# A fused attention and PReLU kernel under a new written order: 1,116 steps, their PSUM banks and the filler matmuls at other places

## The chip, the cores and the metric

The kernel runs on one core of a Trainium2 chip. The core has five engines that work side by side, each through its own instructions in program order: TensorE (PE in the profile, with its weight loads listed apart as PEld), VectorE (DVE), ScalarE (ACT), GpSimd (POOL) and SyncE (SP, which only issues transfers here). They wait for each other through semaphores. Matrix products land in PSUM, a small memory of eight banks; from there DVE or ACT moves them on. The metric is the device time of one execution in microseconds, and lower is better.

## The reference

For each of 8 batches and 8 heads, 512 tokens of width 64 attend to 32 states of the same width, and the states attend to the tokens. Both reads go through one PReLU layer pair of width 2048.

```python
def _attn_ref(x, state):            # x (8,8,512,64), state (8,8,32,64)
    scores = scale * x @ state.T;   a = softmax(scores);   xread = a @ state
    scores2 = scale * state @ x.T;  a2 = softmax(scores2); sread = a2 @ x
    return concatenate([xread, sread], axis=2)
...
    x = attn_out.transpose(0, 2, 1, 3).reshape(B * S, H * D)   # (4352, 512)
    h = x @ w_in                                               # (4352, 2048)
    g = maximum(h, 0) + alpha * minimum(h, 0)
    return g @ w_out                                           # (4352, 512)
```

## The kernel before

The work is cut into nine parts: batches 0 to 7 of 512 tokens each, and part 8, the 256 rows that the states have read. Inputs are turned to f16 on the way in; sums are f32 in PSUM.

**Attention of a batch b.** GpSimd loads x (`lx`, L163). SyncE transposes it by DMA (`xd`, L318); batches 0 and 1 are instead transposed on PE (`xt`) and copied out of PSUM (`xo`, L331). PE forms the scores of all heads (`sc`, L341). From that one PSUM tile DVE takes a block transpose (`sb`, L373) and a row maximum (`tm`, L456), and ACT two exponentials (`te`, L473). The first path is the tokens' softmax: maximum (`smax`), shift (`ssh`, on POOL), exponential (`sexp`), sum (`ssum`), scaling (`snorm`, L440), transpose back (`wb`, L443). The second is the states' softmax: scaling of the exponentials (`tn`, L489 on ACT or L491 on POOL), a DMA transpose by SyncE (`tt`, L495), the product with x on PE (`rd`, L510) and a copy into the rows of part 8 (`rdo`, L521). Batch 0 makes its token softmax from products with paired states instead (`tsc`, L380), in two halves, and transposes it on PE (`at`, L392; copied by `ao`, L395).

**First layer.** The states are multiplied by w_in first (`m`, L537, eight matmuls; copied out by `mo`, L561 or L563). A step `F.b.jc.k` (L590) multiplies that by the softmax weights: two matmuls 512 wide that give 128 of the 2048 hidden columns for all tokens of batch b, in PSUM bank k. ACT takes the negative part (`N`, L643), DVE combines it with the bank into g (`G`, L646), and only then is the bank free again. For part 8, `F` is four matmuls 256 wide (L599). The first two column blocks of batch 0 are done in halves (`f`, L612, `n`, `g`).

**Second layer.** Batch 0 is done plainly (`S`, L660, two matmuls 512 wide; `O` writes out). Parts 1 to 8 use seven products in place of eight for a two-by-two block product: sums of weight quarters (`W`, POOL, L704), sums of halves of g (`U`, POOL, L728, 2.1 us each), products (`P`, L749, four matmuls 256 wide) into three banks per part, partial results kept on the way (`K`, L765) and four quarters sent out (`Q`, L780 and L782, then two transfers by SyncE).

**Start.** DVE writes a pattern (`io`), and PE multiplies it by itself in filler steps (`Z`, L262; the last number counts units of 128 columns) while the first inputs arrive. The states of batch 0 come by `dst`, are turned to f16 by `stc`, transposed on PE into one PSUM tile (`stt`, L275), and that tile is read three times: `sto` (L289, the states as PE will use them) and `sbd.0`, `sbd.1` (L293, the paired states). Weights come in four chunks each (`wi`, `wo`, one transfer a chunk, issued by POOL).

**What sets the order.** Everything follows one text: `ORDER` lists all steps, and a loop at the end of the function calls them one after the other. Each engine runs its instructions in the order in which the list names them, and each queue of transfers likewise. A token gives the step, its batch and indices, then its PSUM banks (0 to 5; scores and some `m` use a further pair) or its engine (`a` ACT, `v` DVE, `p` POOL, `s` SP). So `F.6.2.0` is the first layer of batch 6, column block 2, in bank 0, and `Q.4.0.1.a` a quarter of batch 4 copied by ACT. The list comes from a planner, a program with assumed costs and due times; semaphore waits between the steps are set when the kernel is built, from what each step reads and writes.

Of the kernel before, what the change touches and what calls it, by code (L numbers as in the profile page):

```python
# [34 lines left out]
F.1.4.3 S.0.3.6 mo.1.2.a m.2.2.0.1 sc.2 G.1.6 S.0.3.4 sb.2 tt.0 N.1.4 F.1.8.4 mo.2.2.a.0 S.0.3.7 O.0.0.a mo.2.2.a.1
F.1.0.2 F.1.1.0 S.0.2.1.1 S.0.2.5 S.0.2.3 tm.2 smax.2 N.1.8 N.1.0 O.0.3.a G.1.8 S.0.2.4 nb.2.a S.0.2.6 F.1.13.5 G.1.4
G.1.0 te.2.0 W.3.1.p F.1.9.4 te.2.1 rd.0.3 N.1.1 W.4.0.p N.1.13 N.1.9 rd.1.2 m.3.2 W.4.1.p tsum.2 ssh.p.2 G.1.1
S.0.2.2 sexp.2 G.1.13 rdo.1.a S.0.2.7 S.0.2.0 rdo.0.v ssum.2.5 mo.3.2.a G.1.9 F.1.10.0 P.1.1.1.0.3 O.0.2.a tn.2.1.a
P.1.1.1.1 tn.2.0.a m.2.1 N.1.10 m.2.3.2.4 str.1.1 P.1.1.0.0 snorm.v.2 mo.2.3.a.1 F.1.11.5 lx.3 G.1.10 U.1.3.0.p
mo.2.3.a.0 U.1.1.1.p P.1.1.0.1 P.1.2.1.1.4 N.1.11 wb.2 mo.2.1.a G.1.11 tt.2 F.2.15.2 N.2.15 P.1.2.0.1 F.2.1.0 F.2.14.5  # L40
K.1.1.a sro.1.v P.1.2.1.0 m.3.1 G.2.15 U.1.2.1.p xd.3 N.2.1 m.3.0.1.2 G.2.1 N.2.14 mo.3.1.a P.1.2.0.0 U.1.1.0.p
mo.3.0.a.0 P.1.6.0.1 G.2.14 lx.4 F.2.0.0 N.2.0 U.1.2.0.p F.2.11.5 N.2.11 Q.1.0.0 F.2.2.4 mo.3.0.v.1 U.1.3.1.p
P.1.6.1.1 G.2.0 m.5.0.1.2 rd.2.0 sc.3 G.2.11 N.2.2 mo.5.0.a.0 mo.5.0.a.1 W.3.0.p m.4.0.5.1 G.2.2 P.1.6.0.0 P.1.6.1.0
rdo.2.v sb.3 mo.4.0.a.0 mo.4.0.a.1 K.1.2.a F.2.7.5 N.2.7 U.1.4.0.p tm.3 m.3.3.2.4 F.2.13.0 G.2.7 smax.3 mo.3.3.a.1
# [795 lines left out]
```

## Time and profile before

| | us |
|---|---|
| Median of 3 runs | 211.87 |
| Lowest and highest of them | 210.81, 213.03 |
| The profiled execution | 211.0 |
| Its span, from the first to the last instruction | 209.2 |
| Busy in the span: PE | 201.1 (96%) |
| DVE | 173.1 (83%) |
| POOL | 178.7 (85%) |
| ACT | 150.9 (72%) |
| Fillers on PE, busy | 10.5 |

The profile shows one execution. Rows of its timeline give start, length, engine, line, operation, tiles, shape and a count of instructions taken together; a bracket at the end gives the idle time before the row and who ended it. Matmuls overlap, and the end of each is modelled, so the time that a matmul costs PE is read from start to start of rows that follow each other, not from the lengths. The chain of waits is followed back from the last instruction. A wait is put down to the last semaphore that came, which need not be the whole cause.

### The profile page before, as it was taken

How to read it: one execution, taken by the hardware profiler on the slowest of the kernel's cores; microseconds unless marked ns; L12 is line 12 of the kernel's file. 1: busy time of each engine (PE TensorE's matmuls, PEld its weight loads, DVE VectorE, ACT ScalarE, POOL GpSimd, SP SyncE). 2: the span in 40 equal slices, each digit the busy share in tenths (PEclk: the TensorE clock that was granted, in tenths of full speed). 3: DMA queues.
4: the chain of work that ended last, by engine and by line, in shares of the span. 5: the costliest groups of instructions: out<-in, count | busy, mean ns of one | idle time of the engine just before them, and what ended most of it. 6: DMA issues, size and time to landing. Idle time of an engine off the chain costs nothing.

```text
span 209.2 us, 5084 instructions
## 1 busy us (share of the span) xinstructions
PE 201.1 (96%) x2009; PEld 134.5 (64%) x2009; DVE 173.1 (83%) x263; ACT 150.9 (72%) x295; POOL 178.7 (85%) x112
## 2 busy tenths in 40 slices
...
GB/s 142 190 171 165 205 200 147 211 143 75 218 110 155 48 127 213 22 11 238 199 112 140 113 126 26 3 77 119 109 2 3 125 25 3 50 50 53 115 114 124
DMA packets 44455, 23.43 MB, mean 112 GB/s; under 512 B 23696, under 2 KB 43920, under 8 KB 44432
## 3 DMA queue, kind: packets, MB, share of 16 engines
...
q8 instruction: 15, 0.25, 0.5%
...
## 4 chain that ended last, share of the span: by engine, by line
PE 73%; DVE 9%; DMA 8%; POOL 3%; issue 3%; ACT 2%; SPq 0%; DVEq 0%; POOLq 0%
PE px L749 21%; PE h L590 18%; PE pv L749 10%; PE o L660 6%; PE py L749 6%; DVE g L646 5%; DMA w_out_sb<-in_moe_w_out_dram 4%; PE m_ps L537 4%; PE h L599 3%; PE sr_ps L510 2%; DMA st<-in_state_dram 2%; DMA e2T<-e 2%; POOL gsum L728 2%; DVE nb L456 1%; POOL an L440 1%
## 5 line engine op out<-in xcount | busy, mean ns | idle before, releaser
L646 DVE SCALAR_TENSOR_TENSOR g<-neg,oma_sb,h 128x512 f16<-128x512 f32 (+1 forms) x142 | 94.9, 710 | 13.1 <-ACT neg L643 12.2
L643 ACT ACTIVATE neg<-h 128x512 f32<-128x512 f32 (+1 forms) x142 | 75.9, 583 | 23.8 <-PE h L590 13.3
L590 PE MATMUL h<-aT,m 128*128 128x512 f16 x252 | 66.8, 379 | 1.1 <-ACT oq L780 1.0
L749 PEld LDWEIGHTS <-gsum 128*128 128x128 f16 x480 | 46.5, 98 | 14.4 <-issue 1.5
L749 PEld LDWEIGHTS <-g 128*128 128x128 f16 x360 | 34.7, 98 | 10.5 <-issue 1.7
L728 POOL TENSOR_TENSOR gsum<-g,g 128x1024 f16<-128x1024 f16 (+1 forms) x16 | 32.1, 2009 | 7.1 <-DVE g L646 5.2
L590 PEld LDWEIGHTS <-m 128*128 128x128 f16 x252 | 24.2, 98 | 18.5 <-issue 2.6
L728 POOL TENSOR_TENSOR gsum<-g,gsum 128x1024 f16<-128x1024 f16 (+1 forms) x16 | 31.9, 2006 | 1.4 <-PE px L749 1.2
L728 POOL TENSOR_TENSOR gsum<-gsum,g 128x1024 f16<-128x1024 f16 (+1 forms) x16 | 32.1, 2008 | 1.0
L749 PE MATMUL px<-ws,gsum 128*128 128x256 f16 x240 | 32.1, 273 | 0.0
L728 POOL TENSOR_TENSOR gsum<-g 128x1024 f16<-128x1024 f16 (+1 forms) x16 | 32.1, 2013 | 0.0
L563 ACT CAST m<-m_ps 128x512 f16<-128x512 f32 x36 | 19.7, 596 | 2.7 <-PE m_ps L537 2.5
L765 ACT COPY kept<-px 128x512 f32<-128x512 f32 (+1 forms) x21 | 12.0, 570 | 13.0 <-PE px L749 12.9
L749 PE MATMUL px<-w_out_sb,g 128*128 128x256 f16 x120 | 17.4, 273 | 0.0
L749 PE MATMUL py<-w_out_sb,g 128*128 128x256 f16 x120 | 17.2, 273 | 0.0
L660 PE MATMUL o<-w_out_sb,g 128*128 128x512 f16 x64 | 16.5, 380 | 0.3 <-DMA w_out_sb<-in_moe_w_out_dram 0.3
L749 PE MATMUL px<-w_out_sb,gsum 128*128 128x256 f16 x120 | 16.7, 273 | 0.0
L749 PE MATMUL pv<-ws,gsum 128*128 128x256 f16 x120 | 16.5, 273 | 0.0
L749 PE MATMUL pv<-ws,g 128*128 128x256 f16 x120 | 15.9, 273 | 0.0
L411 POOL TENSOR_TENSOR ts<-ts,mx 128x1024 f32<-128x1024 f32 x7 | 13.4, 1913 | 2.5 <-DVE mx L406 2.5
L782 DVE TENSOR_TENSOR oq<-pv,kept 128x512 f32<-128x512 f32 (+1 forms) x16 | 10.4, 648 | 5.4 <-ACT kept L765 2.8
L561 ACT CAST m<-m_ps 128x1024 f16<-128x1024 f32 x12 | 12.5, 1045 | 0.0
...
## 6 DMA issues: line engine op xcount, KB each, us to landing
...
xg<-in_x_dram POOLq DMA_DIRECT2D x7, 512.0 KB, 6.3
w_in_sb<-in_moe_w_in_dram POOLq DMA_DIRECT2D x4, 512.0 KB, 9.4
w_out_sb<-in_moe_w_out_dram POOLq DMA_DIRECT2D x4, 512.0 KB, 8.4
...
```

Source lines behind the costliest of these rows:

```text
L411: engine(e).tensor_tensor(blocks(cols(live["ts", b], j, S)), blocks(scored(b, j)), over_blocks(cols(live["mx", b], j, S // N)), ALU.subtract,)
L537: nc.tensor.matmul(t[N * k : N * (k + 1), :], st_head(b, h)[64 * r : 64 * r + 64, :], w_in_sb[64 * r : 64 * r + 64, c, 512 * f : 512 * (f ...
L561: copier(e)(m_tile(b, f), t)
L563: copier(e)(m_tile(b, f)[:, g, :], t[g])
L590: nc.tensor.matmul(h_g, ms[b, f][:, g, 128 * j : 128 * (j + 1)], weights(b, g), start=(g == 0), stop=(g == 1),)
L643: nc.scalar.activation(neg, h, RELU, bias=0.0, scale=-1.0)
L646: nc.vector.scalar_tensor_tensor(g_tile(b, jc), negs.pop((b, jc)), oma_sb[:, jc : jc + 1], hs.pop((b, jc)), ALU.mult, ALU.add,)
L660: nc.tensor.matmul(outs[b, q], g_tile(b, jc)[:, 128 * q : 128 * (q + 1)], w_out_sb[:, jc, :], start=not begun and jc == 2 * jc2, stop=left ...
L728: engine(e).tensor_tensor(t, x(), y(), op)
L749: nc.tensor.matmul(pbanks[b, name][:, i, :], of(b, c)[:, j, 128 * i : 128 * (i + 1)], moving[:, 4 * c + j, :], start=not begun and j == 0, ...
L765: copier(e)(t, pbanks[b, "x"])
L782: nc.vector.tensor_tensor(osb, pbanks[b, name], kept[b, add], ALU.add)
```

## The change

Only the text `ORDER` changes; no function does. The planner wrote a new list. Its rules differ in two points: reads of one PSUM bank by different engines are taken to follow each other in program order, and the transfers that GpSimd and SyncE issue are taken to be served as one line. Nearly every step has another place, many another bank. Thirty steps change their engine: 14 go from DVE to ACT, 10 from ACT to DVE, four from ACT to POOL (`cx.0.1`, `tn.2.0`, `tn.2.1`, `tn.4.1`), one from POOL to ACT (`tn.3.0`) and one from POOL to DVE (`snorm.0.0`). The steps themselves are the same set, but for the fillers: eight with 138 units in all become nine with 162. Shown are the stretches that the text below speaks of.

```diff
--- before.py
+++ after.py
 ORDER = """
-dxp.1 io dx.0.0.4.s dx.0.4.8.a id lx.1 mz Z.4.38 dst.s stc.v cx.0.0.v stt.1 cx.0.1.a xt.0.0.1.3 sbd.0.v xt.0.0.0.0
-sbd.1.a xo.0.0.1.a Z.4.9 la sto.v tsc.0.1.5 xo.0.0.0.v tsc.0.0 xt.0.1.1.2 xt.0.1.0.0 smax.0.0 Z.4.15 xo.0.1.0.v
-xo.0.1.1.a tsc.1.1.3 ssh.v.0.0 tsc.1.0 Z.4.16 xt.1.1.1.5 sexp.0.0 smax.0.1 ssh.v.0.1 xt.1.0.0.2 ssum.0.0 xt.1.0.1.1
-lst.0 xt.1.1.0.0 xo.1.0.0.a wi.0 wi.1 sexp.0.1 xo.1.1.1.a xo.1.0.1.v snorm.p.0.0 str.0.3 Z.4.28 xo.1.1.0.v at.0.2
-ssum.0.1 sro.0.a sc.1 m.0.0.5.1 wi.2 snorm.p.0.1 oma.a ao.0.v sb.1 mo.0.0.a.1 m.1.0.0.3 wo.0 tm.1 mo.1.0.a.1
-mo.0.0.a.0 Z.4.21 at.1.1 m.2.0.3.2 mo.1.0.a.0 f.0.0.0.5 ao.1.v mo.2.0.a.0 Z.4.3 mo.2.0.v.1 nb.1.a wo.1 m.0.1.1.3
-n.0.0.0 mo.0.1.a.1 mo.0.1.v.0 f.0.0.1.0 g.0.0.0.1 F.0.3.2 n.0.0.1 g.0.0.0.0 F.0.5.3 F.0.7.1 N.0.3 g.0.0.1.0 wi.3 N.0.5
-g.0.0.1.1 Z.4.8 G.0.3 N.0.7 m.0.2.5.4 mo.0.2.a.0 F.0.2.0 F.0.4.5 G.0.5 wo.2 mo.0.2.a.1 N.0.2 G.0.7 F.0.6.3 W.1.0.p
-G.0.2 N.0.4 F.0.9.4 te.1.1 G.0.4 te.1.0 F.0.10.2 F.0.11.1 N.0.10 N.0.9 smax.1 F.0.8.0 S.0.3.0.5 m.1.1 N.0.11 S.0.3.1
-S.0.3.2 N.0.6 G.0.10 ssh.p.1 G.0.9 N.0.8 S.0.0.0.2 S.0.1.0.4 S.0.1.2 G.0.11 mo.1.1.a S.0.1.1 sexp.1 G.0.8 G.0.6 sc.0.1
-sc.0.0 tm.0 m.0.3.0.1 S.0.0.1 wo.3 ssum.1.3 S.0.3.3 mo.0.3.a.0 mo.0.3.a.1 S.0.0.2 S.0.0.3 tsum.1 nb.0.a lx.2 F.0.14.0
...
-P.2.6.1.1 tn.3.0.p te.4.0 G.3.14 smax.4 N.3.3 P.2.6.0.1 F.3.6.2 K.2.2.a F.3.0.0 N.3.8 U.2.3.1.p P.2.5.0.0 G.3.4 tt.3
-P.2.5.0.1 P.2.5.1.1 N.3.0 P.2.5.1.0 N.3.6 G.3.3 G.3.8 F.3.10.3 te.4.1 N.3.10 sc.5 rd.3.4 G.3.0 F.3.9.5 rdo.3.a
...
-G.4.11 F.4.12.4 F.4.13.2 K.3.1.a G.4.7 N.4.2 F.4.14.0 P.3.6.0.1 N.4.8 N.4.12 sb.5 tt.5 G.4.2 P.3.6.0.0 N.4.14 G.4.8
-G.4.12 P.3.6.1.0 rd.5.1 rd.4.5 m.6.3 U.3.4.1.p rdo.5.a rdo.4.v xd.6 N.4.13 G.4.13 m.7.0.4.1 P.3.6.1.1 mo.7.0.a.1
...
-U.4.3.0.p P.4.7.1.0 tn.6.1.a P.4.7.0.1 G.5.10 F.5.13.4 G.5.9 N.5.5 G.5.5 N.5.6 G.5.6 tn.6.0.a P.4.3.0.0 P.4.7.0.0
-nb.7.a sb.7 F.6.3.1 Q.4.1.1 te.7.1 F.5.4.5 Q.4.0.1.a N.5.13 F.6.2.0 F.6.1.2 N.6.3 P.4.4.0.0 N.5.4 N.6.2 P.4.4.1.0
-U.5.1.0.p G.5.13 P.5.2.1.1.4 G.5.4 G.6.3 te.7.0 tt.6 P.4.4.1.1 U.5.2.0.p P.5.1.1.0.5 F.6.4.1 P.4.4.0.1 G.6.2 P.5.1.0.1
...
-U.5.2.1.p tn.7.1.a F.6.5.2 F.6.12.3 N.6.12 P.5.1.0.0 P.5.2.1.0 K.5.1.a G.6.4 N.6.5 tt.7 F.6.15.1 F.6.9.0 P.5.6.0.0
-G.6.12 ssh.p.7 N.6.15 P.5.6.0.1 G.6.5 N.6.9 F.6.13.3 sexp.7 Q.5.0.0 G.6.9 G.6.15 U.5.3.1.p F.6.6.2 N.6.6 P.5.6.1.0
-rd.6.0 rd.7.4 G.6.6 m.7.1 P.5.6.1.1 rdo.7.a F.6.8.1 rdo.6.a F.8.6.0 K.5.2.a F.6.10.4 ssum.7.2 N.8.6 P.5.5.0.0 N.6.8
...
-P.8.2.0.0.1 U.8.2.0.p U.8.1.1.p P.8.2.0.1 K.8.1.a P.8.6.0.0 Q.7.1.0 U.8.2.1.p P.8.6.0.1 K.8.2.a U.8.3.1.p P.7.3.1.1
-P.7.3.0.1 P.7.3.0.0 Q.8.0.0 P.8.5.0.0 Q.7.0.1.a P.8.5.0.1 P.8.7.0.0.0 U.8.4.1.p K.8.4.v P.8.7.0.1 Q.8.1.1 P.8.3.0.1
-U.8.4.0.p P.8.3.0.0 Q.8.0.1.v P.8.4.0.0 P.8.4.0.1 Q.8.1.0
...
+dxp.1 id lst.0 io dx.0.0.4.s lx.1 Z.0.45 dx.0.4.8.a dst.s stc.a cx.0.0.v stt.2 cx.0.1.p xt.0.0.1.1 xt.0.0.0.3 Z.0.3
+xt.0.1.0.4 xo.0.0.1.a la sto.a mz xt.0.1.1.5 sbd.0.v xo.0.1.0.a sbd.1.v xo.0.1.1.a xo.0.0.0.v tsc.0.1.1 wi.0 tsc.0.0
+Z.0.21 wi.1 tsc.1.1.3 tsc.1.0 str.0.4 smax.0.0 wi.2 ssh.v.0.0 smax.0.1 wo.0 ssh.v.0.1 sexp.0.0 sro.0.a Z.0.25 wo.1
+xt.1.1.0.2 xt.1.0.0.4 sexp.0.1 xo.1.0.0.a xt.1.1.1.3 ssum.0.0 xt.1.0.1.1 xo.1.0.1.a xo.1.1.0.v xo.1.1.1.a snorm.v.0.0
+ssum.0.1 Z.0.15 at.0.5 ao.0.a oma.a wi.3 wo.2 m.1.0.1.4 mo.1.0.v.0 m.0.0.2.3 wo.3 mo.0.0.a.1 snorm.p.0.1 sc.1 Z.0.8
+mo.1.0.a.1 tm.1 mo.0.0.a.0 Z.0.10 at.1.1 sb.1 ao.1.a m.2.0.3.5 mo.2.0.a.0 mo.2.0.v.1 f.0.0.0.4 n.0.0.0 f.0.0.1.1
+g.0.0.0.0 nb.1.a Z.0.20 n.0.0.1 g.0.0.0.1 te.1.1 m.0.1.5.2 F.0.3.3 F.0.2.4 g.0.0.1.0 Z.0.15 g.0.0.1.1 mo.0.1.a.0 N.0.3
+mo.0.1.v.1 G.0.3 te.1.0 N.0.2 F.0.7.5 N.0.7 m.1.1 smax.1 m.0.2.3.2 mo.0.2.a.1 F.0.5.0 mo.0.2.a.0 F.0.4.1 lx.2 F.0.6.2
+G.0.2 N.0.4 N.0.5 ssh.p.1 G.0.7 W.1.0.p N.0.6 F.0.11.3 F.0.9.4 N.0.9 S.0.3.0.5 G.0.4 G.0.5 F.0.10.1 N.0.11 S.0.3.1
+F.0.8.0 W.1.1.p G.0.6 G.0.9 S.0.0.0.2 S.0.0.1 G.0.11 tsum.1 N.0.10 S.0.1.0.4 sexp.1 S.0.0.3 N.0.8 S.0.1.3 S.0.3.3
+mo.1.1.a S.0.1.2 G.0.10 sc.0.1 sc.0.0 G.0.8 m.0.3.1.0 S.0.1.1 S.0.0.2 mo.0.3.a.0 mo.0.3.a.1 S.0.3.2 F.0.14.0 ssum.1.3
+tm.0 tn.1.0.p F.0.15.1 nb.0.a S.0.0.5 lst.1 te.0.0 snorm.v.1 S.0.1.4 xd.2 S.0.3.5 tn.1.1.p N.0.15 wb.1 F.0.12.3 G.0.15
+N.0.14 S.0.3.4 S.0.1.5 te.0.1 G.0.14 tsum.0 F.0.13.1 N.0.12 F.1.7.0 m.1.3 G.0.12 W.2.0.p N.0.13 N.1.7 S.0.1.7 W.3.0.p
...
+tn.3.1.p F.3.3.0 F.3.6.4 smax.4 K.2.2.a F.3.2.5 tt.3 te.4.0 N.3.3 P.2.5.1.0 G.3.7 te.4.1 N.3.6 F.3.0.3 N.3.2 U.2.4.0.p
+G.3.3 U.2.4.1.p P.2.5.1.1 U.2.3.1.p G.3.6 U.2.3.0.p N.3.0 tsum.4 P.2.5.0.0 P.2.5.0.1 K.2.4.a F.3.11.2 rd.3.0 sc.5
...
+G.4.11 U.3.3.1.p tt.5 N.4.10 xd.6 F.4.14.4 N.4.12 P.3.6.1.0 P.3.6.0.0 N.4.14 P.3.6.1.1 G.4.2 rd.4.5 rdo.4.a G.4.12
+rd.5.0 G.4.14 P.3.6.0.1 F.4.6.1 G.4.10 rdo.5.a K.3.2.a m.7.0.0.4 m.6.3 F.4.15.2 smax.5 F.4.13.5 P.3.5.0.0 N.4.6
...
+P.4.7.1.1.3 N.5.10 N.5.6 P.4.5.1.1 tm.7 P.4.7.0.1 K.4.4.a G.5.10 G.5.9 N.5.14 tsum.6 F.5.4.5 nb.7.a P.4.3.1.1
+P.4.7.0.0 te.7.1 P.4.3.1.0 P.4.7.1.0 F.5.13.2 tn.6.0.a U.5.1.0.p G.5.6 G.5.14 wb.6 Q.4.1.1 N.5.13 P.4.3.0.0 G.5.13
+F.6.2.4 F.6.4.1 N.5.4 U.5.2.0.p N.6.2 P.4.3.0.1 G.5.4 Q.4.0.1.a P.4.4.0.1 P.4.4.0.0 P.4.4.1.1 sb.7 N.6.4 te.7.0
+F.6.3.2 G.6.4 P.4.4.1.0 U.5.1.1.p F.6.1.0 N.6.3 F.6.14.1 Q.4.1.0 P.5.1.0.0.5 tn.6.1.a N.6.1 F.6.5.3 G.6.2 P.5.2.0.1.4
+P.5.1.0.1 P.5.1.1.0 N.6.5 tt.6 tsum.7 P.5.2.0.0 smax.7 U.5.2.1.p G.6.5 P.5.1.1.1 U.5.3.1.p G.6.3 P.5.2.1.0 F.6.6.2
+tn.7.1.a G.6.1 P.5.2.1.1 F.6.9.3 tn.7.0.a K.5.1.a F.6.12.0 tt.7 ssh.p.7 N.6.14 N.6.6 Q.5.0.0 N.6.9 G.6.9 P.5.6.0.0
+P.5.6.0.1 G.6.6 N.6.12 P.5.6.1.0 rd.6.3 rd.7.4 m.7.1 rdo.6.a G.6.14 F.6.13.1 sexp.7 P.5.6.1.1 G.6.12 F.6.15.0 K.5.2.a
...
+U.8.3.0.p K.8.1.v P.7.4.0.1 P.8.6.0.0 Q.7.1.0 P.8.6.0.1 P.7.3.1.0 K.8.2.a P.8.2.0.0.3 U.8.4.1.p P.8.5.0.0 P.8.2.0.1
+Q.7.0.1.a P.8.5.0.1 U.8.3.1.p K.8.4.a P.8.7.0.0.2 U.8.4.0.p P.8.7.0.1 Q.8.0.0 P.8.3.0.1 P.8.3.0.0 Q.8.1.1 Q.8.0.1.a
+P.8.4.0.1 P.8.4.0.0 Q.8.1.0
 """
```

More of the change, by code (lines that the diff above doesn't have):

```diff
@@ L35 @@
[L35 to L44, printed above, removed]
@@ new lines @@
+F.1.13.0 F.1.4.3 mo.2.2.a.0 sb.2 F.1.1.5 tm.2 smax.2 rdo.0.a S.0.2.5.4 N.1.0 G.1.0 N.1.4 S.0.2.1 lx.3 F.1.9.1 N.1.13
+S.0.2.0 S.0.2.4 W.4.0.p S.0.2.2 G.1.13 nb.2.a F.1.8.2 S.0.2.7 N.1.1 G.1.4 te.2.0 N.1.9 G.1.1 te.2.1 rd.1.3 m.3.2
+ssh.p.2 N.1.8 m.2.3.5.0 tsum.2 sexp.2 U.1.1.1.p rdo.1.a S.0.2.3 G.1.8 mo.2.3.a.1 tn.2.1.p mo.2.3.a.0 S.0.2.6
+P.1.1.1.0.3 mo.3.2.a F.1.10.0 P.1.1.1.1 P.1.1.0.0 ssum.2.2 snorm.v.2 G.1.9 tn.2.0.p F.1.11.5 xd.3 O.0.2.a N.1.10 wb.2
+N.1.11 U.1.2.1.p m.2.1 G.1.10 str.1.2 G.1.11 tt.2 lx.4 P.1.2.0.1.4 P.1.2.1.1 F.2.15.1 P.1.1.0.1 F.2.1.0 F.2.14.5
```

94 lines of the change are left out of this document (48 added, 46 removed).

## The prediction

> **What bounds the kernel now.** The page comes first: the busy shares, then the chain that ended last.
>
> ```profile
> span 209.2 us, 5084 instructions
> ...
> PE 201.1 (96%) x2009; PEld 134.5 (64%) x2009; DVE 173.1 (83%) x263; ACT 150.9 (72%) x295; POOL 178.7 (85%) x112
> ...
> PE 73%; DVE 9%; DMA 8%; POOL 3%; issue 3%; ACT 2%; SPq 0%; DVEq 0%; POOLq 0%
> ```
>
> PE is busy nearly throughout and carries the chain. But the ends of matmuls are modelled, so the second view is PE's timeline, read from start to start.
>
> ```profile
> 79.96 1.89 PE L590 MATMUL h<-aT,m 128*128 128x512 f16 x8
> 81.69 1.04 PE L749 MATMUL px<-ws,gsum 128*128 128x256 f16 x8
> 82.56 0.81 PE L590 MATMUL h<-aT,m 128*128 128x512 f16 x3
> ```
>
> Eight matmuls 512 wide take 1.73 us (0.216 each), eight of 256 take 0.87 (0.109 each). An `F` or `S` so costs 0.43 and a `P` 0.44. Fillers end at 19.53, the first row below. From there PE keeps this pace to its last matmul, with three breaks of over 0.3 us:
>
> ```profile
> 19.53 0.46 PE L537 MATMUL m_ps<-w_in_sb,stT 64*32 64x512 f16 x8
> ...
> 24.07 0.61 PE L660 MATMUL o<-w_out_sb,g 128*128 128x512 f16 x2
> 24.95 1.24 PE L660 MATMUL o<-w_out_sb,g 128*128 128x512 f16 x5 [0.28 <-DMA w_out_sb<-in_moe_w_out_dram]
> ...
> 102.30 1.47 PE L749 MATMUL px<-ws,gsum 128*128 128x256 f16 x12
> 104.46 1.19 PE L510 MATMUL sr_ps<-e2T,xg 128*64 128x32 f16 x64 [0.69 <-DMA e2T<-e]
> ...
> 136.31 1.24 DVE L373 STREAM_TRANSPOSE ts<-sc 128x1024 f32<-128x1024 f32 x1
> 136.87 1.03 PE L590 MATMUL h<-aT,m 128*128 128x512 f16 x4
> 137.63 0.69 ACT L473 ACTIVATE e<-sc,nb 128x512 f16<-128x512 f32 x1 [1.44 <-issue]
> 138.31 0.58 ACT L780 COPY oq<-px 128x512 f32<-128x512 f32 x1
> 138.94 0.81 PE L590 MATMUL h<-aT,m 128*128 128x512 f16 x3 [1.04 <-ACT oq L780]
> ```
>
> Start to start less the work is idle time: 0.88 - 2 x 0.216 = 0.45 (a chunk of w_out is late); 2.16 - 12 x 0.109 = 0.85 (the transposed exponentials of batch 5 are late); 2.07 - 4 x 0.216 = 1.21. Together 2.5 us. The third shows a rule of this program: `te.7.1` on ACT starts as `sb.7` on DVE ends (136.31 + 1.24 = 137.55), though neither uses what the other makes. Both read the scores' banks, and the one named first in the list goes first. `Q.4.0.1` was queued behind `te.7.1` on ACT, and PE's `F.6.2.0` wanted the bank that `Q.4.0.1` reads.
>
> So the time is: the end of the fillers, plus the matmuls that are then left, plus idle time, plus a tail. The matmuls are the same set in both kernels, and so are the last steps (two products `P.8.4`, `Q.8.1.0`, its transfer). What can differ is how far PE is when the fillers end, and the idle time after.
>
> **The start.** Rows of the timeline, all engines:
>
> ```profile
> 4.30 1.51 POOL L233 DMA_DIRECT2D w_in_sb<-in_moe_w_in_dram  x2
> 4.99 0.62 ACT L189 CAST xg<-x 128x512 f16<-128x512 f32 x1 [2.45 <-DMA x<-in_x_dram]
> 5.92 0.30 PE L275 MATMUL st_ps<-ident,st 128*64 128x128 f16 x4 [0.96 <-DVE st L281]
> 6.15 0.62 PE L326 MATMUL xT_ps<-ident,xg 128*128 128x128 f16 x8
> 6.26 0.28 DVE L293 COPY st_pairs<-st_ps 64x256 f16<-64x256 f16 x1
> 6.58 0.37 ACT L293 COPY st_pairs<-st_ps 64x256 f16<-64x256 f16 x1 [0.97 <-DVE alpha_rows L204]
> 6.98 0.29 DVE L289 COPY stT<-st_ps 128x256 f16<-128x256 f16 x1 [0.39 <-ACT st_pairs L293]
> 7.18 0.41 DVE L331 COPY xT<-xT_ps 128x512 f16<-128x512 f16 x1
> 7.61 0.41 PE L380 MATMUL tsc<-st_pairs,xT 128*128 128x64 f16 x8 [0.35 <-DVE xT L331]
> 7.85 0.61 PE L326 MATMUL xT_ps<-ident,xg 128*128 128x128 f16 x8
> 10.21 1.06 PE L326 MATMUL xT_ps<-ident,xg 128*128 128x128 f16 x16
> 10.85 0.59 ACT L331 COPY xT<-xT_ps 128x512 f16<-128x512 f16 x1 [0.51 <-PE xT_ps L326]
> 11.19 0.58 PE L275 MATMUL st_ps<-ident,st 128*64 128x128 f16 x14
> 11.71 1.69 PE L262 MATMUL fill<-pattern 128*128 128x512 f16 x7
> 13.23 0.39 PE L392 MATMUL at_ps<-ident,an 128*128 128x128 f16 x4
> 13.78 0.62 PE L537 MATMUL m_ps<-w_in_sb,stT 64*32 64x512 f16 x16
> 13.86 1.07 POOL L440 TENSOR_TENSOR an<-ts,r 128x512 f16<-128x512 f32 x1
> 14.32 1.31 PE L262 MATMUL fill<-pattern 128*128 128x512 f16 x6
> ```
>
> The three reads of the states' bank follow each other here too: DVE 6.26 to 6.54, ACT 6.58 to 6.95, DVE from 6.98. The new list puts `sto` first of the three, on ACT, and on ACT behind `xo.0.0.1`. That copy can start at about 6.55 (x is transposed from 6.15, four in 0.245 by the row of 10.21; there the copy came 0.15 after the second four had started and run). So `sto` runs at 7.1 to 7.5 (ACT's small copy took 0.37), then `sbd.0`, `sbd.1` and `xo.0.0.0` follow on DVE at 7.5, 7.75 and 8.0 to 8.4. The second half of `tsc` starts at 8.4; before, it was half of 7.61 to 7.85 later than 7.61, at 7.73. From there on PE has a plain sum. A filler unit is 1.52 us / 28 = 0.054 (11.71 to 13.23):
>
> - `tsc.0.0` 0.12, Z 21 1.13, two `tsc` 0.24, `str` 0.52, Z 25 1.35, sixteen transposes 0.98, Z 15 0.81: to 13.55
> - `at` and `sc` 0.55 (13.23 to 13.78), two `m` 0.54, Z 18 0.97: to 15.6; the second `at` 0.25, `m` 0.27, two `f` of four matmuls 0.88, and 0.1 of waiting for the copy `ao.1`: to 17.1
> - Z 20 1.08, `m` 0.27, two `F` 0.86, Z 15 0.81: to 20.1
>
> The softmax of batch 0 has to keep up. From the second half of `tsc` at 7.73 to the end of its second scaling (13.86 + 1.07) it took 7.2 us; from 8.4 that is 15.6, just when the second `at` wants it. DVE gives two copies `xo` to ACT and gets one scaling, about the same. At 20.1 PE has done one `F` less than at 19.53 before. So the start costs 0.57 + 0.43 = 1.0 us. Bounds: 0 if `tsc` waits no longer than before (then part of the 24 additional filler units, 1.3 us, fills idle time), 2.0 if the softmax slips by another microsecond.
>
> `cx.0.1` moves to POOL, ahead of `wi.0` and all other weights. It can start at 4.99 and takes between 0.62 (ACT's row for the same copy) and 1.07 (POOL's nearest row, an operation with two inputs); I take 1.07, the same engine. `wi.0` is then issued at 6.1 in place of 4.3. Two rows on w_in, the first `wi.0` alone, the second all four chunks:
>
> ```profile
> w_in_sb<-in_moe_w_in_dram POOLq DMA_DIRECT2D x1, 512.0 KB, 8.4
> ...
> DMA to landing us min/median/max: 6.5/9.4/11.1
> ```
>
> With the least, 6.5, it lands at 12.6, with the most at 17.2. Its first user stands at 14.1 in the sum above. Before, its 8.4 held a wait behind x of batch 1; issued later it has less of that, so I take 12.6 to 13.3, and nothing for PE. If that cover is gone, each microsecond late is one on PE. The later chunks are issued without the pauses that POOL's scalings made between them, so w_out comes earlier, and the 0.45 goes.
>
> **The steady part.** `te.7.1` now stands ahead of `sb.7`, and `Q.4.0.1` ahead of `te.7.0`: the 1.21 goes. Next late is `te.7.0`, which waits for `sb.7`, 1.24 at most. Behind it on ACT are `N.6.3`, `tn.6.1` and `N.6.1`; the bank of `F.6.3` is next used at `F.6.6`, four `F` and eight `P` on (5.2 us), so PE doesn't see it. Between `tt.5` and `rd.5` stand one `F`, three `P` and a `rd` (0.43 + 1.31 + 0.6 by the row of 104.46, 2.3 in all) where two `P` stood (0.87): 1.46 more than before, so the 0.85 goes.
>
> The changes of engine between DVE and ACT nearly balance. POOL gets four steps and gives two; those it gets are followed by long cover. POOL also has `lx.2` and the sums `W` earlier, and `tn.0` behind two of them, and on SyncE `tt.0` behind that: from the first `tn.0` to `rd.0` PE has 6.2 us of work (7.6 before), for two scalings and a transpose, 4.8 by the rows further down. So nothing, with 1.4 of cover.
>
> What new idle time comes no row shows. Below nothing it can't be, since PE can't beat its pace. The upper end is the second rival's 3.4 for one mechanism. I take 1.25, half of the old idle time: the causes that made it are rarer here, but the gaps between steps are as close as before.
>
> Profiled execution: 211.0 + 1.0 - 2.5 + 1.25 = 210.75 (its span 209.2 becomes 208.95, with 1.8 around it in both). The median stood 0.87 above the profiled execution: 211.6.
>
> **Rivals.** *Nothing new comes.* For it: each break above has a cause that the new list removes. Against it: the start's 1.0 is mostly filler in the list itself, and the closest gaps, such as two `F` and three `P` (2.2 us) from `F.6.9.3` to `rd.6.3` in its bank, for a product, a pass of ACT and one of DVE, leave no room. 211.87 - 2.5 and 0 to 0.4 for the start: 209.4 to 209.75.
>
> *The transposed exponentials come late.* SyncE issues `tt`, and `rd` on PE waits for it.
>
> ```profile
> L495 SPq DMA_TRANSPOSE e2T<-e x8: 1257/1321/1452, 38.9 to 145.6; - x8
> L491 POOL TENSOR_SCALAR e<-e,r x7: 690/697/711, 32.8 to 98.8; 128x512 f16<-128x512 f16 x7
> ...
> DMA to landing us min/median/max: 3.1/3.4/6.7
> ```
>
> Between `tt` and `rd` PE has 2.6 us of work in batch 3 (four `P`, two `F`), 2.3 in batch 5, and 1.9 in batch 7 (three `P`, a `rd`). If each transpose is issued at its place in the list, with 3.4 to landing PE waits 0.8 + 1.1 + 1.5 = 3.4. With half of the other new idle time: 211.87 + 1.0 - 2.5 + 3.4 + 0.6 = 214.4. Against it: before, in batch 5, 0.87 of work and 0.85 of idle time were enough for 3.4, so the issue ran 1.7 ahead of its place. It decides where landing less that lead passes 3.3. The landings range widely: with 6.7 and no lead the three would wait 13.3. The Trainium skill says in "DMA: Bandwidth & Descriptors", section "Issuing engines are not separate DMA queues", that transfers started by SyncE, ScalarE and GpSimd interleave on the same 16 engines. By that a transpose is late only beside other traffic, and the three stay at 3.4 or under; the spread of the row agrees, though it doesn't say what ran beside the slow one. In the new list a load of x stands right ahead of `tt.4` only, which has over 10 us of work before its `rd`.
>
> *The order doesn't do what it says.* Hand-overs between two readers of a bank remain (`sto` to `sbd.0`, `sb.7` to `te.7.0`). If the second isn't covered, 1.24 more: 212.8.
>
> **The numbers.** A difference under 1% (2.1 us) is about what a measurement of this kernel can't tell from no change. My forecast, between 209.75 and 214.0, has 0.62, and the third rival lies in it. Nothing new has 0.17. Late transposes, or whatever like them adds 2.4 to the forecast, have 0.21. The likeliest time is 211.6. The range goes from 209.4, the end of the first rival, to 214.4, the second's value.
>
> **What would show it.** Right: the second half of `tsc` (L380) at 8.4, waiting for DVE; the last filler ending near 20.1; no idle time before L660 near 25 us, before `sr_ps` of batch 5, or through ACT's copy of `oq` in batch 6. Wrong: fillers that end before 19.3 or after 21, or idle time after them of under 0.3 or over 2.5 us, and for the second rival that it stands before L510.

## The result and the profile after

| | before | after |
|---|---|---|
| Median of 20 runs, us | 211.84 | 211.14 |
| Lowest and highest | 210.59, 213.03 | 209.65, 216.53 |
| Time after over time before, with its 95% interval | | 0.994 (0.991 to 0.997) |
| The profiled execution | 211.0 | 211.87 |
| Its span | 209.2 | 209.4 |

The forecast was 211.6, within 1% of before; 211.14 is that. The ratio leaves out six of the 20 executions of after, which ran at a mean granted clock of 0.982 to 0.994 (the median of the other 14 is 210.1); the runs below show what lowers it. The interval of the ratio lies under 1, so in these runs after is a little faster, by 0.3 to 0.9%.

The page of after, busy shares and chain:

```profile
span 209.4 us, 5101 instructions
...
PE 202.1 (96%) x2016; PEld 135.3 (65%) x2016; DVE 172.5 (82%) x260; ACT 149.7 (71%) x296; POOL 179.6 (86%) x114
...
PE 87%; DMA 10%; SPq 0%; POOL 0%; issue 0%; DVE 0%
PE h L590 25%; PE px L749 25%; PE pv L749 13%; PE o L660 7%; PE py L749 5%; PE m_ps L537 4%; DMA w_in_sb<-in_moe_w_in_dram 4%; DMA e2T<-e 4%; PE h L599 3%; PE sr_ps L510 2%; DMA x<-in_x_dram 2%; PE fill L262 1%; PE sc L341 1%; PE h L612 0%; POOL xg L189 0%; SPq L679 0%
```

DVE's 9% of the chain are gone, POOL and ACT too; what is not PE is now three transfers: the first x, the first chunk of w_in, and one transpose of exponentials (`e2T`). PE's timeline at the places of the three old stops, at the new one, and at the last filler:

```profile
17.45 1.24 PE L262 MATMUL fill<-pattern 128*128 128x512 f16 x5
18.62 0.41 PE L537 MATMUL m_ps<-w_in_sb,stT 64*32 64x512 f16 x8
18.96 1.04 PE L590 MATMUL h<-aT,m 128*128 128x512 f16 x4
...
20.64 0.59 PE L590 MATMUL h<-aT,m 128*128 128x512 f16 x2
...
25.19 0.59 PE L590 MATMUL h<-aT,m 128*128 128x512 f16 x2
25.62 1.67 PE L660 MATMUL o<-w_out_sb,g 128*128 128x512 f16 x7
...
60.27 0.40 PE L341 MATMUL sc<-xT,stT 64*32 64x256 f16 x16
61.89 0.68 PE L510 MATMUL sr_ps<-e2T,xg 128*64 128x32 f16 x32 [1.22 <-DMA e2T<-e]
...
103.94 1.47 PE L749 MATMUL px<-ws,gsum 128*128 128x256 f16 x12
105.34 1.19 PE L510 MATMUL sr_ps<-e2T,xg 128*64 128x32 f16 x64
...
138.28 1.03 PE L590 MATMUL h<-aT,m 128*128 128x512 f16 x4
139.15 0.60 PE L749 MATMUL px<-w_out_sb,gsum 128*128 128x256 f16 x4
```

Start to start, the rows near 25, 105 and 138 us carry only their work (0.43, 1.40 and 0.87): the three old stops are gone. One new one stands before `rd.2.0`: 61.89 - 60.27 = 1.62, less the 0.33 that `sc` takes (60.27 to 60.60 in the first experiment) 1.29. The last filler ends at 20.64, 1.1 later than before.

The new stop begins with two transfers. Their issues, from the timeline, and then all transfers issued from 54 to 55 us (KB each, us to landing):

```profile
54.03 0.95 POOL L163 DMA_DIRECT2D xg<-in_x_dram  x1
...
54.32 1.30 SPq L495 DMA_TRANSPOSE e2T<-e  x1
```

```profile
xg<-in_x_dram POOLq DMA_DIRECT2D x1, 512.0 KB, 7.5
out_dram<-osb SPq DMA_DIRECT2D x1, 256.0 KB, 2.4
e2T<-e SPq DMA_TRANSPOSE x1, 7.4
```

GpSimd's `lx.4` left 0.29 us ahead of SyncE's `tt.2`. The load landed at 61.5, the transpose at 61.7. All eight transposes, in the view of their tile, show how far it stands out:

```profile
DMA to landing us min/median/max: 3.1/3.2/7.4
```

### The profile page after: what moved, and what is told of

Same layout as the page of the kernel before. It is cut to its first block, busy times and chain, and to the rows that moved or that the text cites. A ratio compares the mean times of both kernels' runs of the same rounds, so it can differ in the third digit from the quotient of the medians.

```text
span 209.4 us, 5101 instructions
## 1 busy us (share of the span) xinstructions
PE 202.1 (96%) x2016; PEld 135.3 (65%) x2016; DVE 172.5 (82%) x260; ACT 149.7 (71%) x296; POOL 179.6 (86%) x114
## 4 chain that ended last, share of the span: by engine, by line
PE 87%; DMA 10%; SPq 0%; POOL 0%; issue 0%; DVE 0%
PE h L590 25%; PE px L749 25%; PE pv L749 13%; PE o L660 7%; PE py L749 5%; PE m_ps L537 4%; DMA w_in_sb<-in_moe_w_in_dram 4%; DMA e2T<-e 4%; PE h L599 3%; PE sr_ps L510 2%; DMA x<-in_x_dram 2%; PE fill L262 1%; PE sc L341 1%; PE h L612 0%; POOL xg L189 0%; SPq L679 0%
## 5 line engine op out<-in xcount | busy, mean ns | idle before, releaser
L563 ACT CAST m<-m_ps 128x512 f16<-128x512 f32 x35 | 19.4, 601 | 5.7 <-PE m_ps L537 5.6
L765 ACT COPY kept<-px 128x512 f32<-128x512 f32 (+1 forms) x19 | 11.0, 578 | 14.5 <-PE px L749 14.4
L749 PE MATMUL px<-w_out_sb,gsum 128*128 128x256 f16 x120 | 17.5, 273 | 0.0
L749 PE MATMUL px<-w_out_sb,g 128*128 128x256 f16 x120 | 16.9, 273 | 0.0
L749 PE MATMUL py<-w_out_sb,g 128*128 128x256 f16 x120 | 16.7, 273 | 0.0
L262 PE MATMUL fill<-pattern 128*128 128x512 f16 (+3 forms) x44 | 11.7, 406 | 1.1 <-DVE pattern L216 1.1
```

The source lines that it names most:

```text
L262: nc.tensor.matmul(live["fill"][:, : 128 * w].rearrange("p (a c) -> p a c", c=128), pattern, pattern.unsqueeze(1).to_broadcast([128, w, 128]),
L563: copier(e)(m_tile(b, f)[:, g, :], t[g])
L749: nc.tensor.matmul(pbanks[b, name][:, i, :], of(b, c)[:, j, 128 * i : 128 * (i + 1)], moving[:, 4 * c + j, :], start=not begun and j == 0, ...
L765: copier(e)(t, pbanks[b, "x"])
```

## The experiments

**The load moved back.**

```diff
-... G.1.11 tt.2 lx.4 P.1.2.0.1.4 ... sc.3 rd.2.0 mo.5.0.a.0 ...
+... G.1.11 tt.2 P.1.2.0.1.4 ... sc.3 rd.2.0 lx.4 mo.5.0.a.0 ...
```

> The kernel after with one step moved: lx.4 (GpSimd's load of x of batch 4) stands right behind rd.2.0 in place of right behind tt.2. In the profile of after GpSimd issued this load at 54.03 us, 0.29 ahead of SyncE's tt.2 at 54.32; the load landed at 61.53 and tt.2 at 61.76, and PE stood 1.29 us before rd.2.0 at 61.89. Theory A (the transpose waits its turn behind the load on the shared transfer engines): tt.2 lands 3.0 to 3.5 us after its issue, rd.2.0 follows sc.3 without a stop, the span falls by 1.3 to about 208.1, and the median by 0.5 to 1.3 (it is not the whole 1.3 if some executions of after issue the two in the other order already). Theory B (tt.2 is late because it is issued late, tn.2.0 and tn.2.1 having gone from ACT to GpSimd): tt.2 still takes 5 us or more beside xd.3 and O.0.2, and at least 0.5 of the stop stays. xd.4 and sc.4 have more than 8 us to spare and should not move.

The same window of its profile, and PE's rows:

```profile
e2T<-e SPq DMA_TRANSPOSE x1, 3.1
```

```profile
60.27 0.40 PE L341 MATMUL sc<-xT,stT 64*32 64x256 f16 x16
60.60 0.68 PE L510 MATMUL sr_ps<-e2T,xg 128*64 128x32 f16 x32
```

The transpose was issued at 54.23, nearly as late as in after, with the same output transfer ahead of it, and took 3.1; the stop is gone. So it was the load, not the late issue. Theory A holds. The median was 210.24 (before, beside it: 212.07), the ratio 0.992 (0.988 to 0.995). That is below the 0.994 of after, but the intervals overlap.

**`te.7.1` ahead of `sb.7`, in the kernel before.**

```diff
-nb.7.a sb.7 F.6.3.1 Q.4.1.1 te.7.1 F.5.4.5 Q.4.0.1.a ...
+nb.7.a te.7.1 sb.7 F.6.3.1 Q.4.1.1 F.5.4.5 Q.4.0.1.a ...
```

> The kernel before with one step moved: te.7.1 stands ahead of sb.7 in place of behind Q.4.1.1. Theory of the prediction: PE's stop of 1.21 us at F.6.2.0 (before: 138.94, put down to ACT's copy oq) comes from ACT, whose te.7.1 waits for sb.7 on DVE because both read one pair of banks; with the two exchanged ACT does not wait, the stop goes, and the span falls by 1.0 to 1.2 unless DVE, whose sb.7 now waits for te.7.1, is late for a bank next. Rival: ACT is simply behind (its passes N and copies pile up there), the stop stays above 0.8 or moves to the next F by the same amount, and the time stays within 0.3 us of before.

Its timeline, PE and DVE:

```profile
137.36 1.89 PE L590 MATMUL h<-aT,m 128*128 128x512 f16 x8
139.41 0.81 PE L749 MATMUL pv<-ws,g 128*128 128x256 f16 x6 [0.15 <-DVE oq L782]
```

```profile
137.53 1.25 DVE L373 STREAM_TRANSPOSE ts<-sc 128x1024 f32<-128x1024 f32 x1 [0.65 <-ACT e L473]
```

The stop of 1.21 at `F.6.2.0` is gone (it is among the eight matmuls of 137.36). Now DVE's `sb.7` waits 0.65 for ACT's `te.7.1`: the pair follows the list in this direction too. 0.32 came back at the next product (139.41 - 137.36 - 1.73), which waited for DVE. Time 210.84 against 212.07, ratio 0.994 (0.992 to 0.997); the medians of the spans are 208.85 and 210.0. The theory holds, with its price.

**Two groups of fillers taken out of after.**

```diff
-g.0.0.0.0 nb.1.a Z.0.20 n.0.0.1 ... g.0.0.1.0 Z.0.15 g.0.0.1.1 ...
+g.0.0.0.0 nb.1.a n.0.0.1 ... g.0.0.1.0 g.0.0.1.1 ...
```

> The kernel after without its last two groups of filler matmuls (Z.0.20 and Z.0.15, 35 of the 162 units; what they write is never used). Theory of the prediction (fillers are plain PE time on the path): the fillers' 1.9 us (35 x 0.054) leave the start and the time falls by 1.5 to 1.9. Rival (they stand where PE would wait anyway, for the weight chunks that land every 2.5 us or for DVE and ACT): idle time of 1.4 to 1.9 us comes in their place before 31 us, and the time changes by less than 0.5. Weight chunks w_in 2 at 19.2 and w_out 1 at 24.3 should be the first to be late: m.0.2 would be reached at 19.3 and the first product with w_out 1 at about 24.2.

```profile
16.36 1.05 PE L612 MATMUL h<-aT,m 128*128 128x256 f16 x8
17.99 0.41 PE L537 MATMUL m_ps<-w_in_sb,stT 64*32 64x512 f16 x8 [0.58 <-DVE m L563]
18.33 1.53 PE L590 MATMUL h<-aT,m 128*128 128x512 f16 x5
20.15 0.39 PE L590 MATMUL h<-aT,m 128*128 128x512 f16 x1 [0.29 <-DVE m L563]
20.64 0.62 PE L537 MATMUL m_ps<-w_in_sb,stT 64*32 64x512 f16 x16
```

The rival holds. Of the 1.9 us, 0.74 + 0.27 + 0.73 = 1.74 stands as idle time at three places, two of them put down to the copies `mo` (L563), which PE meets sooner; not to the weights, which I had expected to be late first. The ratio was 0.991 (0.988 to 0.995), against 0.994 for after; the intervals overlap. So the fillers here are hardly a price: they fill time in which PE would wait.

**The loads of alpha moved back.**

```diff
-xt.0.1.0.4 xo.0.0.1.a la sto.a ... str.0.4 smax.0.0 ...
+xt.0.1.0.4 xo.0.0.1.a sto.a ... str.0.4 la smax.0.0 ...
```

> The kernel after with one step moved: la (a memset on DVE and four small strided loads of alpha by SyncE) stands behind str.0, about 4 us later, so that the loads leave SyncE at about 8.5 in place of 4.84 to 6.20. In after lx.1 landed at 11.57 and w_in chunk 0 at 14.10; before, with la issued at 6.61 to 7.95, lx.1 landed at 9.64 and the chunk at 12.75. Theory A (GpSimd's loads go one behind another, each landing as the last one is through, and la's many small packets slow the line): lx.1 lands at 10.7 or earlier, chunk 0 2.5 us behind it at 13.3 or earlier, the 0.43 us that PE stood before the first m goes, and the time falls by 0.4. Theory B (the line is slower because lst.0 now stands ahead of lx.1; la costs nothing): lx.1 lands at 11.3 to 11.8, chunk 0 at 13.9 to 14.3, and the 0.43 stays. In both oma may come later (before: la landed at 12.4 for it); if it is late the halves of batch 0's PReLU show it behind 17 us.

`lx.1` landed at 10.18 and chunk 0 at 12.87, so the 0.43 before the first `m` was gone, as Theory A has it. But with `la` in its old place the two also landed at 10.69 and 13.08 (the load moved back), and at 10.17 and 12.68 (its repetition, below). So neither theory is shown: the late landings come and go between executions, and why stays open. And the last filler ended at 20.54 all the same. The ratio was 0.996 (0.993 to 0.998). The run gave something else: here `lx.4` left 0.16 ahead of `tt.2`, which then took 6.7, and the stop was 0.41.

**After once more.**

> The kernel after itself, once more, beside the next three on one chip, so that they can be compared with it directly. Its stop before rd.2.0 was 1.29 us where GpSimd's lx.4 left 0.29 ahead of SyncE's tt.2, and 0.41 in another kernel with the same steps there (la later), where it left 0.16 ahead (tt.2 then took 6.70 in place of 7.43). If the stop differs so between executions, the spans of this kernel spread over 1 us or more (207.8 to 209.5), and a profile shows any stop from 0 to 1.6. If it stands in every execution, the spans lie 1.0 to 1.3 above those of the next kernel.

```profile
59.88 0.40 PE L341 MATMUL sc<-xT,stT 64*32 64x256 f16 x16
62.08 0.68 PE L510 MATMUL sr_ps<-e2T,xg 128*64 128x32 f16 x32 [1.80 <-DMA e2T<-e]
```

Here the load left 0.46 ahead and the stop was 1.87. The six executions took 211.57 to 213.56, median 213.21, against 211.78 for before; four of them had a mean clock of 0.987 to 0.992. Ratio 1.004 (1.000 to 1.009): the kernel that was level with before, or a little faster, is here a little slower, and that by the four: the two at full clock took 211.57 and 211.64, level with before. The stop differs between executions, and these spans (209.6 to 211.4) lie above what was expected; the clock comes below.

**The read moved back, the load left where it is.**

```diff
-... sc.3 rd.2.0 mo.5.0.a.0 ... P.1.6.1.0 G.2.2 U.1.4.0.p P.1.6.0.0 tm.3 ...
+... sc.3 mo.5.0.a.0 ... P.1.6.1.0 G.2.2 U.1.4.0.p P.1.6.0.0 rd.2.0 tm.3 ...
```

> The kernel after with one step moved: rd.2.0 stands five steps later, behind m.3.3, P.1.6.1.0 and P.1.6.0.0 (0.5 + 0.44 + 0.44 = 1.4 us of PE work) in place of right behind sc.3; the load lx.4 and the transpose tt.2 stay as they are. Theory A (the stop is only the late transpose, and cover is worth as much as an earlier landing): tt.2 still takes 6.5 to 7.5 us where lx.4 leaves ahead of it, PE does not stand for it (at most 0.2), and the time is that of the kernel with the load later, 0 to 1.3 below after by how often after has its stop. Rival: the copy rdo.2 on DVE or the next user of bank 0, F.2.5.0, comes late in its place, and the time stays that of after.

```profile
xg<-in_x_dram POOLq DMA_DIRECT2D x1, 512.0 KB, 8.1
...
e2T<-e SPq DMA_TRANSPOSE x1, 8.0
```

```profile
61.27 1.05 PE L749 MATMUL px<-ws,gsum 128*128 128x256 f16 x8
62.25 0.68 PE L510 MATMUL sr_ps<-e2T,xg 128*64 128x32 f16 x32
```

The transpose takes 8.0 here, and PE does not stand for it: `rd.2.0` starts at 62.25, behind two products from 61.27, which is their work and 0.11; the transpose landed at 62.15, just in time. 0.56 of small stops came in its place at `m.3.3`. Median 210.5, ratio to before 0.993 (0.989 to 0.997); after on the same chip had 213.21, and 211.6 in its two executions at full clock. Theory A holds: cover is worth nearly what the earlier landing is.

**The kernel before with its three stops mended.**

```diff
-... wi.0 wi.1 sexp.0.1 ... m.0.0.5.1 wi.2 snorm.p.0.1 ... m.1.0.0.3 wo.0 tm.1 ... nb.1.a wo.1 m.0.1.1.3
+... wi.0 wi.1 wi.2 wo.0 wo.1 sexp.0.1 ... m.0.0.5.1 snorm.p.0.1 ... m.1.0.0.3 tm.1 ... nb.1.a m.0.1.1.3
-P.3.6.1.0 rd.5.1 rd.4.5 m.6.3 U.3.4.1.p rdo.5.a rdo.4.v xd.6 N.4.13 G.4.13 m.7.0.4.1 P.3.6.1.1 mo.7.0.a.1
+P.3.6.1.0 rd.4.5 m.6.3 U.3.4.1.p rdo.4.v xd.6 N.4.13 G.4.13 P.3.6.1.1 rd.5.1 rdo.5.a m.7.0.4.1 mo.7.0.a.1
-nb.7.a sb.7 F.6.3.1 Q.4.1.1 te.7.1 F.5.4.5 ...
+nb.7.a te.7.1 sb.7 F.6.3.1 Q.4.1.1 F.5.4.5 ...
```

> The kernel before with its three stops mended and nothing else: w_in chunk 2 and w_out chunks 0 and 1 issued right behind w_in chunk 1; rd.5 behind rd.4, m.6.3 and one more product (1.3 us of cover more); te.7.1 ahead of sb.7. The prediction summed the three at 0.45 + 0.85 + 1.21 = 2.5 us; the third alone gave 1.15 of the span's median, with 0.32 of a new stop at P.4.4.0.0. Theory: the three add up, the time falls by 2.0 to 2.5 (ratio 0.988 to 0.991), to a span of about 207.7; and since the start of the list of before is kept, which the prediction held to be 1.0 cheaper and the profile of after showed 1.5 cheaper, it ends 0.5 to 1.5 below after without its stop. Rival 1: the stops come back in part further on (as 0.32 of the third did), and the time falls by 1.2 to 1.8. Rival 2: the start of before is not cheaper over many executions (its fillers ended at 19.5 in one profile and at 20.1 in another), and this kernel ends level with after without its stop.

```profile
103.59 0.68 PE L510 MATMUL sr_ps<-e2T,xg 128*64 128x32 f16 x32 [0.22 <-DVE g L646]
...
106.31 0.40 PE L537 MATMUL m_ps<-w_in_sb,stT 64*32 64x512 f16 x4 [0.21 <-ACT XS L521]
```

All three stops are gone, and 1.3 of the 2.5 came back in others: 0.39 and 0.61 around the moved `rd` (its bank was not yet free, and its copy held the bank of the next `m`), 0.31 behind `te.7.1`. Time 210.58 against 211.78, ratio 0.995 (0.991 to 0.999). Rival 1 holds, at the lower end of its 1.2 to 1.8. The start is the cheaper one: the last filler ended at 19.45, and the mended kernel is nearly as fast as after without its stop (0.993 and 0.992 above) in spite of the 1.3.

**Chunk 0 of w_in issued earlier.**

```diff
-... lx.1 Z.0.45 ... tsc.0.1.1 wi.0 tsc.0.0
+... lx.1 wi.0 Z.0.45 ... tsc.0.1.1 tsc.0.0
```

> The kernel after with one step moved: wi.0 stands right behind lx.1, ahead of GpSimd's cast cx.0.1, so that it leaves GpSimd at about 4.4 us in place of 5.4 to 5.7. Theory A (GpSimd's loads are served one behind another: in five profiles chunk 0 landed 2.4 to 2.7 us behind the load ahead of it whenever it was issued): it lands 2.4 to 2.7 behind lx.1, at 12.8 to 14.1, as before. Theory B (the price is per transfer from its issue, 7.2 to 8.7): it lands a microsecond earlier, at 11.6 to 13.1, and no more than 2.0 behind lx.1. The cast comes 0.7 later, and with it the transposes of x of batch 0, the scores tsc and the end of the fillers by up to 0.5.

GpSimd's timeline (`lx.1` had left at 3.42), then `lx.1` and chunk 0 in the view of transfers, with their time to landing:

```profile
4.31 0.87 POOL L233 DMA_DIRECT2D w_in_sb<-in_moe_w_in_dram  x1
```

```profile
xg<-in_x_dram POOLq DMA_DIRECT2D x1, 512.0 KB, 8.0
w_in_sb<-in_moe_w_in_dram POOLq DMA_DIRECT2D x1, 512.0 KB, 9.7
```

Issued 1.1 us earlier than in after (5.43), chunk 0 landed at 14.0, 2.5 behind `lx.1` (in after: 14.1, and 2.5 behind). Theory A: the place in GpSimd's line sets the landing, not the time of issue; this rests on one execution. It took 213.64, and not for its start (the last filler ended at 20.54): its stop before `rd.2.0` was 1.86, and the granted clock of PE behind that stop (start:end, us, PE busy, clock, share of the transfer engines, GB/s) was:

```profile
62.00:63.00 1.00, 0.64 (x40) 1.00 0.23 78
63.00:64.00 1.00, 1.00 (x16) 0.86 0.88 167
64.00:66.00 2.00, 2.00 (x15) 0.50 1.27 93
66.00:68.00 2.00, 2.00 (x10) 0.72 0.42 94
```

A mean of 0.86 over 1 us is 0.28 us at 0.50, and 0.72 over 2 us is 1.12: with the 2.0 between 3.4 us at half the clock. PE lost 1.6 us by it: from 62.36 to 68.81 it did what took 61.89 to 66.77 in after, 6.45 us for 4.88.

**The load moved back, repeated; then with the paired states first.** The second has, on top of the first:

```diff
-xo.0.0.1.a la sto.a mz xt.0.1.1.5 sbd.0.v xo.0.1.0.a sbd.1.v xo.0.1.1.a xo.0.0.0.v tsc.0.1.1
+xo.0.0.1.a la mz xt.0.1.1.5 sbd.0.v xo.0.1.0.a sbd.1.v sto.a xo.0.1.1.a xo.0.0.0.v tsc.0.1.1
```

> The first experiment's kernel again (after with lx.4 behind rd.2.0), beside the next two on one chip as their measure. Expected: no stop before rd.2.0, spans of 207.8 to 208.8, and no stretch of a lower granted clock.

> The kernel of the run before this one with one more step moved: sto (ACT's copy of the states) stands behind sbd.0 and sbd.1 (DVE's two copies from the same bank) in place of ahead of them. In three of its like DVE stood 1.95 to 2.3 us for sto, and PE 0.44 to 0.99 before the scores tsc. Theory of the prediction (reads of one bank follow each other as the list names them, and PE's start is a plain sum behind tsc): sbd.0 starts at about 6.5 in place of 7.1 to 7.5, PE's stop before tsc falls under 0.2, the last filler ends 0.5 to 0.9 earlier (at 19.7 to 20.0), and the time falls by 0.5 to 0.9. Rival: the fillers cover waits that the copies of ACT and DVE set (as the run without the last two groups showed), w_in chunk 0 lands at 13.0 and stops the first m, and the last filler ends less than 0.3 earlier, with the same time.

DVE and PE of the first, then the same of the second:

```profile
7.58 0.59 DVE L293 COPY st_pairs<-st_ps 64x256 f16<-64x256 f16 x2 [2.45 <-ACT stT L289]
...
8.32 0.66 PE L380 MATMUL tsc<-st_pairs,xT 128*128 128x64 f16 x8 [0.83 <-DVE st_pairs L293]
...
20.68 0.59 PE L590 MATMUL h<-aT,m 128*128 128x512 f16 x2
```

```profile
6.33 0.59 DVE L293 COPY st_pairs<-st_ps 64x256 f16<-64x256 f16 x2 [1.22 <-PE st_ps L275]
...
7.29 0.43 PE L380 MATMUL tsc<-st_pairs,xT 128*128 128x64 f16 x8
...
19.53 0.59 PE L590 MATMUL h<-aT,m 128*128 128x512 f16 x2
```

The first repeats: 210.32 against 212.24, ratio 0.992 (0.989 to 0.994), spans 207.8 to 208.7. In the second, DVE waits for the transposed states alone, PE does not stand before `tsc`, and the last filler ends at 19.53 in place of 20.68. Time 209.46, ratio 0.988 (0.985 to 0.990), spans 206.9 to 208.0. The theory holds. This is the fastest kernel here, ahead of before and of after.

**A longer stop on purpose.** Also on top of the first:

```diff
-... G.1.11 tt.2 P.1.2.0.1.4 ... F.2.0.0 Q.1.0.0 U.1.3.1.p ... rd.2.0 lx.4 mo.5.0.a.0 ... rdo.2.v U.1.3.0.p F.2.13.1
+... G.1.11 P.1.2.0.1.4 ... F.2.0.0 Q.1.0.0 tt.2 U.1.3.1.p ... rd.2.0 mo.5.0.a.0 ... rdo.2.v U.1.3.0.p lx.4 F.2.13.1
```

> The kernel two runs before with a stop made on purpose: tt.2 stands behind Q.1.0.0, so that SyncE issues it at about 60.2 us and it lands at about 63.2, and lx.4 stands further back yet so that nothing runs ahead of it. PE should stand 2.4 to 3.0 us before rd.2.0. In four profiles with a stop there of 1.29, 1.57, 1.86 and 1.87 us the second and third were followed by some 3.3 us at a granted clock of 0.50, which cost 1.6 us more, the first and the last were not. Theory (the clock follows how busy PE was over a stretch of about that length, so a longer stop trips it more often): most executions show a mean clock of 0.985 to 0.993, the profile a stretch at 0.50 behind the stop, and the time is 4 to 4.6 us above the kernel without the stop. Rival (the lower clock has nothing to do with the stop): mean clock 0.996 to 1.0 in most executions, and the time is 2.4 to 3.0 above.

The same columns as above:

```profile
61.00:63.00 2.00, 0.00 (x0) 1.00 0.84 185
...
64.00:65.00 1.00, 1.00 (x41) 0.94 0.08 16
65.00:68.00 3.00, 3.00 (x19) 0.50 0.36 33
68.00:70.00 2.00, 2.00 (x12) 0.93 1.42 193
```

PE stood 2.9 us, and then ran 0.12 + 3.0 + 0.28 = 3.4 us at 0.50. Of six executions five had a mean clock of 0.988 to 0.992 and one of 1.0; median 214.56, 4.2 above the kernel without the stop. The one at full clock had a span of 211.0, 2.6 above the other kernel's median of 208.4, the five others 212.3 to 213.0. The theory holds in what it forecast; how the chip sets the clock no run here shows.

## Why the prediction was right, and where not

A change of less than 1% came out, and nearly the number, but the number in part by luck. The profiled execution took 1.1 us more than forecast, and the median, which was to stand 0.87 above it, stood 0.73 below: two errors that offset each other. And one term, the new idle time, had the right size without the reason.

| Step | predicted | profile of after |
|---|---|---|
| Start (last filler, and one `F` fewer done) | 20.1: +1.0 | 20.64: +1.54 |
| Old idle time | -2.5 | -2.5 |
| New idle time | +1.25 | +1.29 |
| Span | 208.95 | 209.4 (209.5 by the rows above) |
| Around the span | 1.8 | 2.5 |
| Profiled execution | 210.75 | 211.87 |
| Median, from the profiled execution | +0.87: 211.6 | -0.73: 211.14 |

**The old idle time** is right in all three places, for the reasons named. The rule that two readers of a bank follow the list is shown by its undoing: exchange the two, and the other engine waits. Behind `te.7.0` the predicted cover held: ACT stood 0.41 for `sb.7`, PE nothing.

**The start** was taken for a plain sum behind the second half of `tsc`, at 8.4 because DVE's copies stand behind `sto`. That mechanism is shown: DVE waited 1.95 for it in after (first row below), 2.45 in the repetition, and with the copies first the last filler ended 1.15 earlier. In the profile of after the second half ran at about 8.0 (`sto` came 0.5 sooner than I had it), in the repetition near 8.5. PE's own stop ahead of `tsc` was 0.83 for these copies in the repetition; in the profile of after it was 0.68 (up to 7.18), and ended with the landing of a load of x, so there the copies were not the only thing that was late. What was off is the size of the sum behind it, 12.6 us for 11.7: 0.43 is a wait for chunk 0 (second row below), the rest many small terms (eight matmuls of `m` take 0.34, from 18.62 to 18.96, where I took 0.27; 20 filler units 1.17, from 17.45, where I took 1.08). "Nothing for PE" failed for chunk 0 in this execution: it landed at 14.1, where I had 12.6 to 13.3, since `lx.1` ahead of it landed late. In six other profiles with this start it landed at 12.7 to 13.1 five times, and once at 14.0. That `cx.0.1` took 0.61 in place of the 1.07 I had, and `wi.0` left at 5.43 in place of 6.1, made no difference to that.

```profile
7.04 0.59 DVE L293 COPY st_pairs<-st_ps 64x256 f16<-64x256 f16 x2 [1.95 <-ACT stT L289]
...
14.15 0.62 PE L537 MATMUL m_ps<-w_in_sb,stT 64*32 64x512 f16 x16 [0.43 <-DMA w_in_sb<-in_moe_w_in_dram]
```

In eight profiles with the start of after (in two of them `la` or `wi.0` moved) the last filler ended between 20.25 and 20.96, in three with that of before between 19.45 and 20.06: some 1.0 and the `F`, so 1.4 in place of 1.0.

"The start's 1.0 is mostly filler in the list itself" was weak too: taken out, 35 units leave 1.74 of their 1.9 us behind as idle time. In two experiments on the start, this one and the one with the pairs first, PE had mainly waited for copies of DVE and ACT.

**The new idle time** has the predicted size, but not for the predicted reason. I had no place for it and took half of the old; it stood in one place, and was the second rival's mechanism in a batch that the rival had not named. The sentence that failed is "In the new list a load of x stands right ahead of `tt.4` only". `lx.4` stands right behind `tt.2`, but the two are issued by different engines, and GpSimd was ahead of SyncE. The gaps in batches 3, 5 and 7 that I priced were no stops: the three transposes took 3.2, 3.3 and 3.1, with no load of GpSimd under way (SyncE's own transfers were). By the rule weighed there (the Trainium skill, "DMA: Bandwidth & Descriptors", section "Issuing engines are not separate DMA queues": transfers share the same 16 engines and interleave) a transpose is late only beside other traffic, and the traces agree; the failure was in looking for that traffic in the order of the list alone. The trace of before could have told: "it doesn't say what ran beside the slow one" is true of the row, but the slow one (6.7) is `tt.4`, issued at 94.19 while the load `lx.6` was under way (91.42 to 97.63), and the next (5.0) is `tt.2`, issued at 51.56 beside `lx.3` (47.74 to 53.66).

Nor is the 1.29 in every execution. Eleven of the 20 have spans of 207.7 to 208.8 at a mean clock of 0.997 or more, which are the spans of the kernel without the stop (207.8 to 208.8 in its twelve executions). No trace shows them, so that they lack the stop is inferred; but then the match of 1.29 with 1.25 is one execution's, and luck.

**The last step** added 0.87 because the median of before stood so far above its profile. For after it stood 0.73 below: its profiled execution had a stop of 1.29 and 0.7 more than usual around its span. One execution's distance from the median said nothing of the next kernel's.

The range and the chances hold for this comparison. The second one (213.21) would still lie in the range, at its upper end, by the second rival's mechanism and the lower clock of four of its six executions. That a stop can be followed by half the clock was in none of the cases.
